# Moving a gate's sine and last multiplication into the even step of a pair of tiles

## Chip, cores and metric

One core of one Trainium2 chip runs the whole program. The metric is device time in microseconds (us) of one execution, as the median of several; lower is better. All data is float32.

## What is computed

The program is a cross attention between tokens and a small recurrent state, and behind it a two-layer network whose activation is h * cos(h). Cut to what matters:

```python
# x: (8, 8, 512, 64), state: (8, 8, 32, 64)
a  = softmax(scale * x @ state.T);  xread = a @ state
a2 = softmax(scale * state @ x.T);  sread = a2 @ x
y  = concat(xread, sread)                 # (8, 8, 544, 64)
y  = y.transpose(0, 2, 1, 3).reshape(4352, 512)
h  = y @ w_in                             # w_in: (512, 2048)
g  = h * cos(h)
out = g @ w_out                           # w_out: (2048, 512)
```

## The kernel before

**Tiles and steps.** The hidden layer is made in tiles of 128 hidden features by 512 tokens of one batch: 16 tiles `f` for each of the 8 batches `b`, and 16 smaller ones at the end for the state rows of all batches. One tile is one *step*; step 32 is tile 0 of batch 2. Steps 0 to 31 (batches 0 and 1) are ordered by a planner of their own. Everything from step 32 on is issued by the loop that starts at line 1676, which calls `later_pair` (line 1631) for each step, and it is this part that the change touches. Each engine works through its own queue strictly in the order in which the program issued the instructions; the order of the statements in `later_pair` therefore is the order of the work. A period is 32 steps (two batches), and its issue pattern repeats: 32 to 63, 64 to 95, 96 to 127.

**Hidden tiles in pairs, seven products.** Two neighbouring tiles (an even step and the odd one after it) form a pair and are made together by a Strassen-like scheme: seven products in place of eight, `seven_part` (line 531). A pair's seven products are issued as parts 0 to 3, two steps ahead of their use: at an even step TensorE (PE) does part 0 and part 1 of the *coming* pair, at the odd step part 2 and part 3. Behind part 0 ScalarE (ACT) makes two copies (lines 528, 529). VectorE (DVE) adds one sum after part 1 and one after part 2 (`seven_sum`, line 551; called the first and the second sum here). Part 2 can't start before the first sum is done, part 3 not before the second. There are two double banks of PSUM, so the coming pair is written where the pair before the current one was: its part 0 has to wait until that pair's last multiplication has read the bank.

**The gate.** h * cos(h) of a pair takes four instructions, each 128 x 1024: `gate` (ACT, line 564) rounds to an integer, `gate2` (DVE, line 567) subtracts, `gate3` (ACT, line 570) takes the sine, `gate4` (DVE, line 584) multiplies by h and writes to `g_all`. One buffer `q_all` carries all four, so the next pair's `gate` waits for this pair's `gate4`. Before the change `gate` and `gate2` stand in the even step, `gate3` and `gate4` in the odd one.

**The rest of a step.** Between the parts PE does one or two *stages* (`multiply`, line 772: eight matmul records for the output product, itself a seven-product scheme named p1 to p7 in stages 0 to 6), each followed by copies on ACT (lines 780, 781, 787) or sums on DVE (783, 789, 607). GpSimd (POOL) makes the sums of activations which these products read (`Product.sums`, `outer_sum`, line 715) and the sums of weight columns which part 0, 1 and 2 read (`sw_sums`, line 521). The *outer sums* that combine rows of activations are split between DVE and POOL; rows of the four blocks are numbered 0 to 3.

**Attention work between.** `plan(b)` puts the attention of the next batch and the *state products* (`products`, line 312, into the PSUM banks `at`, copied by ACT at line 462 to `sw_all`) into steps 0 to 15 of a batch: `go(0)` issues the PE part, `go(1)` and `go(2)` ACT copies, `go(3)` and `go(4)` DVE work, `go(5)` the exponentials. State products of a batch are made at its steps 0, 3, 8 and 12, `scores` (again into `at`) at step 4, `spread2` and `norm1` (DVE lines 373, 374, 332, 393) at step 8 and `halves` (DVE, line 507) at steps 12 and 13.

The names and lines that the change and the steps of the prediction touch: `later_pair` 1631 to 1673; `plan` 972 to 1015; the loop's outer sums 1699 and 1700; `gate` 564, `gate2` 567, `gate3` 570, `gate4` 584; `seven_copies` 528 and 529; `seven_sum` 551; `products_kept` 462.

Of the kernel before, what the change touches and what calls it, by code (L numbers as in the profile page):

```python
# [22 lines left out]
def kernel(  # L23
# [8 lines left out]
    nc = tc.nc  # L32
# [6 lines left out]
    NF = Dff // P  # L39
# [28 lines left out]
    QT, NQUAD = 4, 12  # L68
    g_all = consts.tile([P, (NQUAD + 1) * QT, S], F32)
    TEMPS = 4  # L70
    quads_free = [11]

    def quad(n):
        return g_all[:, QT * n:QT * n + QT]
# [392 lines left out]
    def part(b, name, *args):  # L467

        if b not in attn:
            attn[b] = Attention(b)  # L470
        getattr(attn[b], name)(*args)
        if (name, args) == ("reads", (1,)) and b + 1 < B:
            if b > 0:
                attn[b + 1] = Attention(b + 1)
                loads_due.extend(attn[b + 1].load_tokens())
            loads_due.extend(load_x(b + 1))
# [5 lines left out]
    def hidden(t):  # L482
        if t.paired:
            t.hp = h_pairs[t.at][:, t.f % 2, 0:t.n]
        else:
            t.hp = single_pool.tile([P, S], F32, name="h1")
        for i in range(t.kn):
            nc.tensor.matmul(out=t.hp, lhsT=t.lhs(i), rhs=t.rhs(i),  # L488
                             start=(i == 0), stop=(i == t.kn - 1))
# [8 lines left out]
    def seven(t):  # L498
        return t.pair is not None and t.b > 1
# [48 lines left out]
    def seven_sum(t, k):  # L548
        h1, h2 = [h_pairs[t.at][:, i] for i in range(2)]
        o = (h1, h2)[k][:, HI]  # L550
        nc.vector.tensor_tensor(o, h2[:, LO], sums_all[:, 0], op=ALU.add)  # L551
# [7 lines left out]
    def gate(t):  # L559
        t.q = q_all[:, t.f % 2, 0:t.n]  # L560
        if t.paired:
            t.hp = h_pairs[t.at][:, :, 0:t.n]
            t.q = q_all[:, :, 0:t.n]
        nc.scalar.activation(t.q.bitcast(I32), t.hp, func=ACTF.Copy, bias=0.25)  # L564

    def gate2(t):
        nc.vector.tensor_tensor(t.q, t.q.bitcast(I32), t.hp, op=ALU.subtract)  # L567

    def gate3(t):
        nc.scalar.activation(t.q, t.q, func=ACTF.Sin, bias=halfpi,  # L570
                             scale=-TWO_PI)

    def gate4(t):
        row = t.row
        if t.i // QT == len(quads_of[row]):
            quads_of[row].append(quads_free.pop(0))
        t.slot = QT * quads_of[row][t.i // QT] + t.i % QT
        t.g = g_all[:, t.slot, 0:t.n]
        g = t.g
        if t.paired:  # L580
            t.mate.slot = t.slot + 1
            t.mate.g = g_all[:, t.slot + 1, 0:t.n]
            g = g_all[:, t.slot:t.slot + 2, 0:t.n]
        nc.vector.tensor_tensor(g, t.hp, t.q, op=ALU.mult)  # L584
# [125 lines left out]
    def sub(engine, o, x1, x2):  # L710
        n = max(1, S // o.shape[2])
        if engine is nc.vector:
            n = o.shape[1]
        for i in range(0, o.shape[1], n):
            engine.tensor_tensor(o[:, i:i + n], x1[:, i:i + n], x2[:, i:i + n],  # L715
                                 op=ALU.subtract)
# [253 lines left out]
    warm(WARM, a0.xp[3])  # L970

    def plan(b):
        pe, x_act, y_act, x_dve, y_dve, z_act = [
            {s: [] for s in range(NF)} for _ in range(6)]

        def prod(s, b, nt, *bank):
            pe[s].append((b, "products", nt) + bank)
            x_act[s].append((b, "products_kept", nt) + bank)

        def pairs(s, b, name, kept, i):  # L980
            pe[s] += [(b, name, i), (b, name, i + 1)]
            x_act[s].append((b, kept, i))
            y_act[s].append((b, kept, i + 1))

        def early(b, s):
            for k in range(NK):
                to = (x_dve, y_dve)[k % 2]
                to[s[k // 2]].append((b, "tokens_turned", k))
            pe[s[2]].append((b, "scores"))
            x_dve[s[2]].append((b, "max1"))  # L990
            x_dve[s[3]].append((b, "spread1"))
            y_dve[s[3]].append((b, "shift"))
            y_dve[s[4] - 1].append((b, "max2"))
            z_act[s[4]].append((b, "exps"))
            y_dve[s[4]].append((b, "sums1"))
            x_dve[s[5]].append((b, "spread2"))
            y_dve[s[5]].append((b, "norm1"))

        def late(b, s):
            pairs(s[0], b, "turn", "turn_kept", 0)  # L1000
            pe[s[1]].append((b, "reads", 0))
            pe[s[2]].append((b, "reads", 1))
            x_dve[s[2]].append((b, "keep"))
            pe[s[3]].append((b, "keep2"))
            x_act[s[3]].append((b, "keep3"))

        if b:
            prod(0, b, 1)
            prod(3, b, 2)
            prod(8, b, 3)  # L1010
            if b + 1 < B:
                prod(12, b + 1, 0)
                early(b + 1, (1 + (b == 1), 2 + (b == 1), 4, 5, 7, 8, 9))
                late(b + 1, (9, 10, 11, 15))
        return pe, x_act, y_act, x_dve, y_dve, z_act


    all_tiles = list(tiles())
# [45 lines left out]
    def outer_sum(engine, n, o, x1, x2, half, i):  # L1064
        o, x1, x2 = [quad(quads_of[n, r][half])[:, 2 * i:2 * i + 2]
                     for r in (o, x1, x2)]
        sub(engine, o, x1, x2)
# [42 lines left out]
    def go(n):  # L1110
        for p in todo[n]:
            part(*p)
# [513 lines left out]
    def names_raw(i):  # L1626
        h = i % 2
        n = (2 * h, 2 * h + 1) if i < 4 else range(QT)
        return " ".join(f"Q{SLOTS[i]}_{k}" for k in n)

    def later_pair(step, t, ahead):
        coming = ahead[0] if ahead and ahead[0].paired else None
        seven_ = coming is not None and seven(coming)
        first = coming if even or coming is None else coming.mate
        if not t.paired:
            hidden(t)
        if even or not t.paired:
            gate(t)
        else:
            gate3(t.mate)  # L1640
            go(5)
        if seven_:
            seven_part(first, 0 if even else 2)
        elif coming is not None:
            hidden(coming)
        if even or not t.paired:
            gate2(t)
        if t.b == 1 and s in (13, 14):
            halves(2, s - 13)
        if seven_ and not even:  # L1650
            seven_sum(first, 1)
        if not t.paired:
            gate3(t)
        if not t.paired:
            gate4(t)
        elif not even:
            gate4(t.mate)
        if even:
            stages(step, 1)
        go(0)  # L1660
        if not even:
            stages(step, 1)
        if seven_:
            seven_part(first, 1 if even else 3)
            if even:
                seven_sum(first, 0)
        go(1)
        go(3)
        if t.pair is None and not even:
            state_sums(t.mate)  # L1670
            state_sums(t)
        go(2)
        go(4)

    first_pair()
    for step, t in enumerate(all_tiles[FIRST:], FIRST):
        s, even = step % NF, step % 2 == 0
        if s == 0 and t.b < B:
            steps = plan(t.b)
        todo = [p[s] if t.b < B else [] for p in steps]  # L1680
        while stores_due:
            stores_due.pop(0)()
        for u in all_tiles[step + 3:step + 4]:
            if seven(u) and u.f % 2 == 0:
                sw_sums(u)
        now[0] = step
        while totals_due and totals_due[0][0] <= step:
            totals_due.pop(0)[1]()
        if step == PERIOD:
            singles.__exit__(None, None, None)  # L1690
            pool2 = ctx.enter_context(tc.tile_pool(name="hps2", bufs=1,
                                                   space=PSUM))
            h_pairs[0] = pool2.tile([P, 2, S], F32, name="h2")
        later_pair(step, t, all_tiles[step + 2:step + 3])
        if later and later[0][0] <= step:
            later.pop(0)[1]()
        for what in weights_at[step]:
            what()
        for what in outer_at[step]:
            outer_sum(*what)  # L1700
        for pd, k in sums_at[step]:
            pd.sums(k)
        if t.b < B - 1 and t.b > 1 and s in (12, 13):
            halves(t.b + 1, s - 12)
        stages(step)
        load_now(H if step < NF else 4)
        if step == PERIOD * (B // 2) - 8:
            load_end_weights(2)
        if t.pair is None and t.n_th > 3 and len(quads_free) > 2:
            load_end_weights(1)  # L1710
# [36 lines left out]
```

## Time and profile before

| quantity | value |
|---|---|
| median of 3 runs | 740.53 us (739.6 to 740.9) |
| the profiled execution: its own time | 740.65 us |
| its span, first to last instruction | 738.9 us |
| PE matmul busy | 708.2 us, 96% |
| PE weight loads busy | 519.0 us, 70% |
| POOL busy | 542.5 us, 73% |
| DVE busy | 506.8 us, 69% |
| ACT busy | 347.3 us, 47% |
| mean granted TensorE clock | 0.993 |

The rows of the four gate instructions for pairs (48 each): line 564 ACT 1029 ns, line 567 DVE 1216 ns, line 570 ACT 1151 ns, line 584 DVE 1217 ns. A seven-product sum (line 551) is 430 ns, an outer sum on DVE (line 715, 128 x 1024) 1490 ns, a copy of a state product (line 462) 590 ns, a POOL sum of 128 x 512 1349 ns.

How to read it: the page gives busy time of each engine for the whole span, then in 40 slices, then a chain of work followed back from the end. The matmul records of PE overlap: a record of 256 columns lasts 381 ns on average, but eight of them follow each other in 1.73 us, so the distance from start to start is 0.22 us. A pause of less than about 0.2 us is thus not seen as idle time, and pauses have to be read from the start times in the timeline.

A step is found in the timeline by its `gate` (line 564, ACT, 128 x 1024), one for each even step: step 32 at 165.0 us, 36 at 185.1, 40 at 205.5, 42 at 214.8, 52 at 264.2, 60 at 302.1, 64 at 321.0, 72 at 363.2, 96 at 478.5, 116 at 579.3.

### The profile page before, as it was taken

How to read it: one execution, taken by the hardware profiler on the slowest of the kernel's cores; microseconds unless marked ns; L12 is line 12 of the kernel's file. 1: busy time of each engine (PE TensorE's matmuls, PEld its weight loads, DVE VectorE, ACT ScalarE, POOL GpSimd, SP SyncE). 2: the span in 40 equal slices, each digit the busy share in tenths (PEclk: the TensorE clock that was granted, in tenths of full speed). 3: DMA queues.
4: the chain of work that ended last, by engine and by line, in shares of the span. 5: the costliest groups of instructions: out<-in, count | busy, mean ns of one | idle time of the engine just before them, and what ended most of it. 6: DMA issues, size and time to landing. Idle time of an engine off the chain costs nothing.

```text
span 738.9 us, 10734 instructions
## 1 busy us (share of the span) xinstructions
PE 708.2 (96%) x3626; PEld 519.0 (70%) x3626; DVE 506.8 (69%) x703; ACT 347.3 (47%) x586; POOL 542.5 (73%) x524
## 2 busy tenths in 40 slices
PE   8898889999999999999999999999999999999997
PEld 3343343477778878777778788777688788888886
DVE  4989979957866668849756577768665467355550
ACT  5799675654463446343634464344634533211110
POOL 1557789375998997588998665879989665799600
PEclk9999999999999999999999999999999999999999
DMA  9966799536346964693238635762225466456662
GB/s 297 285 192 193 236 265 301 122 96 150 87 128 117 214 172 115 142 197 86 82 80 168 160 96 116 147 154 83 75 68 119 115 205 143 108 156 203 155 152 46
DMA packets 204021, 111.33 MB, mean 151 GB/s; under 512 B 149888, under 2 KB 166784, under 8 KB 203968
## 3 DMA queue, kind: packets, MB, share of 16 engines
q1 hardware_dynamic: 202880, 110.14, 57.4%
q8 instruction: 29, 0.48, 0.3%
q10 hardware_dynamic: 960, 0.39, 0.2%
q14 instruction: 24, 0.20, 0.1%
q0 software_dynamic: 128, 0.13, 0.1%
HBM read 87.03 MB, written 23.59 MB: 150 GB/s over the span
## 4 chain that ended last, share of the span: by engine, by line
PE 59%; POOL 21%; DVE 9%; issue 3%; DMA 3%; ACT 2%; SPq 1%; ACTq 0%; POOLq 0%; DVEq 0%
PE o L772 29%; POOL g_all L715 16%; PE h L543 13%; PE h L488 8%; POOL swS_all L521 3%; PE at L312 3%; PE at L877 2%; DMA held<-in_state_dram 2%; PE o L640 2%; POOL sw_all L521 2%; DVE g_all L715 1%; PE at L417 1%; DVE q_all L567 1%; DVE g_all L232 1%; DVE g_all L584 1%
## 5 line engine op out<-in xcount | busy, mean ns | idle before, releaser
L715 POOL TENSOR_TENSOR g_all<-g_all 128x512 f32<-128x512 f32 x252 | 332.5, 1349 | 61.8 <-DVE g_all L715 40.4
L772 PE MATMUL o<-g_all 128*128 128x256 f32 x1456 | 343.7, 381 | 2.4 <-POOL g_all L715 2.4
L772 PEld LDWEIGHTS o<-g_all 128*128 128x128 f32 x1456 | 273.7, 190 | 49.7 <-issue 5.7
L567 DVE TENSOR_TENSOR q_all<-q_all,h 128x1024 f32<-128x1024 int32 (+1 forms) x88 | 85.3, 971 | 40.7 <-ACT q_all L564 40.4
L564 ACT ACTIVATE q_all<-h 128x1024 int32<-128x1024 f32 (+1 forms) x88 | 73.1, 833 | 81.2 <-PE h L543 35.1
L584 DVE TENSOR_TENSOR g_all<-h,q_all 128x1024 f32<-128x1024 f32 (+1 forms) x88 | 85.7, 973 | 24.5 <-ACT q_all L570 23.6
L570 ACT ACTIVATE q_all<-q_all,halfpi 128x1024 f32<-128x1024 f32 (+1 forms) x88 | 84.2, 957 | 38.7 <-DVE q_all L567 38.5
L551 DVE TENSOR_TENSOR h<-h,sums_all 128x256 f32<-128x256 f32 x96 | 41.3, 430 | 77.5 <-PE h L543 60.2
L488 PE MATMUL h<-aT_all,sw_all 128*128 128x512 f32 x128 | 64.0, 628 | 13.0 <-DVE g_all L584 12.3
L543 PE MATMUL h<-aT_all,sw_all 128*128 128x256 f32 x192 | 59.6, 392 | 3.8 <-DVE g_all L584 3.4
L543 PE MATMUL h<-aS_all,swS_all 128*128 128x256 f32 x192 | 60.2, 395 | 2.6 <-ACT sums_all L529 1.8
L715 DVE TENSOR_TENSOR g_all<-g_all 128x1024 f32<-128x1024 f32 x42 | 62.0, 1490 | 0.1
L543 PE MATMUL h<-aS_all,sw_all 128*128 128x256 f32 x192 | 58.0, 384 | 0.1
L488 PEld LDWEIGHTS h<-aT_all,sw_all 128*128 128x128 f32 x128 | 23.2, 195 | 44.3 <-issue 21.5
L521 POOL TENSOR_TENSOR swS_all<-sw_all 128x128 f32<-128x128 f32 x48 | 22.5, 468 | 41.8 <-ACT sw_all L462 41.8
L543 PEld LDWEIGHTS h<-aS_all,swS_all 128*128 128x128 f32 x192 | 33.9, 189 | 27.0 <-issue 12.1
L780 ACT COPY o<-o 128x256 f32<-128x256 f32 x26 | 9.3, 357 | 85.1 <-PE o L772 85.1
L543 PEld LDWEIGHTS h<-aT_all,sw_all 128*128 128x128 f32 x192 | 34.5, 189 | 16.3 <-DVE g_all L584 12.2
L237 POOL TENSOR_TENSOR w_in<-w_in,aS_all 128x1024 int32<-128x1024 int32 (+1 forms) x10 | 22.3, 2241 | 29.9 <-DVE w_in L232 27.2
L787 ACT COPY o<-sums_all 128x256 f32<-128x256 f32 x26 | 9.8, 378 | 68.2 <-PE o L772 68.2
L543 PEld LDWEIGHTS h<-aS_all,sw_all 128*128 128x128 f32 x192 | 35.6, 190 | 8.2 <-DVE h L551 2.7
L607 DVE SCALAR_TENSOR_TENSOR held<-o,held 128x512 f32<-128x512 f32 x38 | 25.9, 681 | 13.7 <-PE o L772 13.1
(116 smaller groups left out, 931.6 us busy)
## 6 DMA issues: line engine op xcount, KB each, us to landing
g_all<-blocks_kept SPq DMA_DIRECT2D x206, 256.0 KB, 2.8
blocks_kept<-g_all SPq DMA_DIRECT2D x48, 256.0 KB, 3.9
g_all<-in_moe_w_out_dram SPq DMA_DIRECT2D x8, 1024.0 KB, 5.7
out_dram<-ot SPq DMA_DIRECT2D x128, 64.0 KB, 2.0
g_all<-in_moe_w_in_dram SPq DMA_DIRECT2D x6, 1024.0 KB, 7.1
x_b<-in_x_dram SPq DMA_DIRECT2D x24, 256.0 KB, 4.7
xT<-in_x_dram SPq DMA_DIRECT2D x80, 64.0 KB, 2.8
x_b<-in_x_dram SPq DMA_DIRECT2D x16, 128.0 KB, 4.3
```

Of the source, the lines that this page charges most:

```text
L237: nc.gpsimd.tensor_tensor(bits, bits, e, op=ALU.add)
L488: nc.tensor.matmul(out=t.hp, lhsT=t.lhs(i), rhs=t.rhs(i), start=(i == 0), stop=(i == t.kn - 1))
L521: nc.gpsimd.tensor_tensor(o, x1, x2, op=op)
L543: nc.tensor.matmul(out=out_, lhsT=w, rhs=r, start=start, stop=True, skip_group_check=True)
L551: nc.vector.tensor_tensor(o, h2[:, LO], sums_all[:, 0], op=ALU.add)
L564: nc.scalar.activation(t.q.bitcast(I32), t.hp, func=ACTF.Copy, bias=0.25)
L567: nc.vector.tensor_tensor(t.q, t.q.bitcast(I32), t.hp, op=ALU.subtract)
L570: nc.scalar.activation(t.q, t.q, func=ACTF.Sin, bias=halfpi, scale=-TWO_PI)
L584: nc.vector.tensor_tensor(g, t.hp, t.q, op=ALU.mult)
L607: nc.vector.scalar_tensor_tensor(out=out.t[:, ch], in0=bank, scalar=TWO_PI, in1=b.t[:, ch], op0=ALU.mult, op1=ALU.add)
L715: engine.tensor_tensor(o[:, i:i + n], x1[:, i:i + n], x2[:, i:i + n], op=ALU.subtract)
L772: nc.tensor.matmul(out=o, lhsT=ring[(self.first + k) % NB][:, i], rhs=g[:, i], start=(start and i == 0), stop=(i == QT - 1), skip_group_ch ...
```

## The change

The sine and last multiplication of a pair move from the odd step into the even one, behind part 1 and the first sum of the coming pair, provided that the coming pair is one of the seven-product kind and that a buffer for the result is at hand (`fits`). They do not move at steps 32, 40, 48 and 52, nor for the last pair before the state tiles (126) and in the state tiles. Where they move, DVE's outer sums that read row 3 are put off from the even step to the odd one, behind the second sum (in every period one such sum of step 2 and one of step 4 of the period). ACT's copies of state products made at an odd step (tile 3 of each batch) move to the next step, behind that step's `gate` and seven-product copies.

In the emitted program PE, POOL and the DMA queues keep their order; only DVE and ACT are reordered. The number of instructions is the same, activation table loads included. Since `gate4` takes its buffer one step earlier, some buffers of `g_all` are handed out in another order.

```diff
@@ plan
         def prod(s, b, nt, *bank):
             pe[s].append((b, "products", nt) + bank)
-            x_act[s].append((b, "products_kept", nt) + bank)
+            (w_act[s + 1] if s % 2 else x_act[s]).append(
+                (b, "products_kept", nt) + bank)
@@ later_pair
+        early = t.paired and seven_
         if even or not t.paired:
             gate(t)
         else:
-            gate3(t.mate)
+            if not t.mate.gated:
+                gate3(t.mate)
             go(5)
         if seven_:
             seven_part(first, 0 if even else 2)
...
         if even or not t.paired:
             gate2(t)
+        go(6)
...
         elif not even:
-            gate4(t.mate)
+            if not t.mate.gated:
+                gate4(t.mate)
+            while sums_late:
+                outer_sum(*sums_late.pop(0))
         if even:
             stages(step, 1)
         go(0)
...
             seven_part(first, 1 if even else 3)
             if even:
                 seven_sum(first, 0)
+        fits = t.pair is not None and (t.i % QT > 0 or len(quads_free) > 1)
+        t.gated = even and early and fits
+        if t.gated:
+            gate3(t)
+            gate4(t)
         go(1)
         go(3)
@@ the loop over steps
         for what in outer_at[step]:
-            outer_sum(*what)
+            if t.gated and what[0] is nc.vector and 3 in what[2:5]:
+                sums_late.append(what)
+            else:
+                outer_sum(*what)
```

More of the change, by code (lines that the diff above doesn't have):

```diff
@@ L972, in plan @@
     def plan(b):
-        pe, x_act, y_act, x_dve, y_dve, z_act = [
-            {s: [] for s in range(NF)} for _ in range(6)]
+        pe, x_act, y_act, x_dve, y_dve, z_act, w_act = [
+            {s: [] for s in range(NF)} for _ in range(7)]
         def prod(s, b, nt, *bank):
             pe[s].append((b, "products", nt) + bank)
-            x_act[s].append((b, "products_kept", nt) + bank)
+            (w_act[s + 1] if s % 2 else x_act[s]).append(
+                (b, "products_kept", nt) + bank)
         def pairs(s, b, name, kept, i):
@@ L1014, in plan @@
                 late(b + 1, (9, 10, 11, 15))
-        return pe, x_act, y_act, x_dve, y_dve, z_act
+        return pe, x_act, y_act, x_dve, y_dve, z_act, w_act
     all_tiles = list(tiles())
@@ L1629, in names_raw @@
         return " ".join(f"Q{SLOTS[i]}_{k}" for k in n)
+    sums_late = []
     def later_pair(step, t, ahead):
```

## The prediction, made before the changed kernel ran

> **What bounds the kernel now.** I read the slices first (PE at nine tenths from step 32 on), then the waits, then the chain of waits between 173 and 218 us, then the timeline of four places. PE is full by the page, but its records overlap, so I took start-to-start distances above 0.22 us as pauses. PE starts of part 0 that come late behind `gate4` (line 584) are the pauses the change aims at:
>
> ```profile
> PE h L543 <- DVE g_all L584: 3.4, 8, 0.4
> PEld h L543 <- DVE g_all L584: 12.2, 24, 0.8
> ACT q_all L564 <- DVE g_all L584: 28.2, 9, 5.2
> ```
>
> The columns are total us, times, longest. The second row, weight loads, counts overlapped time as well, so I don't add it. From the timeline, part 0 is late by 0.18, 0.28, 0.59, 0.09, 0.59, 0.10 and 0.59 us in the first period (steps 34, 36, 38, 40, 42, 54, 62), by 0.19, 0.27, 0.59, 0.59, 0.59 in the second (66, 68, 70, 74, 94), by 0.19, 0.28, 0.59, 0.59 in the third: 6.3 us in all, 0.8% of the span. That is the most this change can remove by its main idea, and about 0.1 us more for each, which the trace shows PE to lose on restarting after a pause.
>
> Most of these lie in steps 34 to 42 of a period, where POOL and DVE are full as well. The chain there:
>
> ```profile
> 176.75 6.87 POOL g_all L715 x4
> ...
> 204.46 10.83 POOL g_all L715 x8
> 215.29 0.42 POOL swS_all L521
> 215.71 0.04 issue
> 215.75 0.70 PE h L543 x2
> ```
>
> POOL works from 176.75 to 215.71 without a pause and PE then waits for its weight sums: in the first period POOL sets when step 42 goes on, whatever DVE does. POOL's start at 176.75 waits for DVE's first outer sum of step 33.
>
> At the end of a period, steps 60 to 62, the bound is DVE alone (its rows of the timeline):
>
> ```profile
> 304.45 1.22 DVE L567 TENSOR_TENSOR q_all<-q_all,h 128x1024 f32<-128x1024 int32 x1
> ...
> 307.14 1.22 DVE L715 TENSOR_TENSOR g_all<-g_all 128x1024 f32<-128x1024 f32 x1
> 308.27 0.42 DVE L507 TENSOR_TENSOR aS_all<-aT_all 128x256 f32<-128x256 f32 x1
> 308.73 1.37 DVE L507 TENSOR_TENSOR aS_all<-aT_all,aS_all 128x256 f32<-128x256 f32 x1
> 310.02 0.68 DVE L607 SCALAR_TENSOR_TENSOR held<-o,held 128x512 f32<-128x512 f32 x1
> 310.62 0.42 DVE L551 TENSOR_TENSOR h<-h,sums_all 128x256 f32<-128x256 f32 x1
> 310.96 1.21 DVE L584 TENSOR_TENSOR g_all<-h,q_all 128x1024 f32<-128x1024 f32 x1
> ```
>
> DVE is full; part 3 (PE 311.10) waits for the second sum (310.62 to 311.04), then part 0 of step 62 (PE 312.22) for `gate4`. And step 52, where the scores (line 312) need the banks that the moved copies (line 462) empty:
>
> ```profile
> 263.27 1.07 ACT L462 COPY sw_all<-at 128x512 f32<-128x512 f32 x2
> ...
> 264.21 1.06 ACT L564 ACTIVATE q_all<-h 128x1024 int32<-128x1024 f32 x1
> 265.13 0.41 ACT L528 COPY h<-h 128x256 f32<-128x256 f32 x1
> ...
> 265.57 0.37 ACT L529 COPY sums_all<-h 128x256 f32<-128x256 f32 x1
> ...
> 265.64 1.09 PE L312 MATMUL at<-xT,st_all 64*32 64x512 f32 x16
> ```
>
> **What the Trainium skill says.** "SBUF — State Buffer", section Who interferes with whom: a DVE instruction with two SBUF inputs contends with a GpSimd one that reads SBUF, and one blocks fully. The trace agrees: POOL's 128x512 sums take 1.27 us alone and 2.19 to 2.26 beside a DVE outer sum or `norm1`. The number of such meetings does not change, so I price this at nothing, with 1 us either way in the range. "ScalarE: Activation LUTs", What ACT_TABLE_LOAD costs: about 1283 ns; the trace has 1.28 us. No load is added, but those at steps 56, 72, 88, 104 now stand in front of a sine that DVE needs a step earlier (taken at its 1.28 us). "Perfetto Trace Analysis", Identifying the Most-Contended Engine: matmul busy share is a poor measure; hence the start distances.
>
> **The change part by part.** I walk the queues with the trace's durations: in a full DVE queue one instruction costs about 1.13 us for a gate part, 0.33 for a seven-product sum, 0.6 for 128x512, 1.1 to 1.4 for an outer sum.
>
> *First period, steps 34 to 42.* POOL's start hangs on step 33, whose pair isn't moved, and its run is full: 0. (If DVE got later than POOL, a loss of up to 0.5.)
>
> *Second and third period, steps 64 to 74* (times of the second). `gate4` of step 64 moves to step 64, so the token transposes of step 65 follow its second sum at 330.3 in place of 332.0, and the outer sum that starts POOL comes 1.6 us earlier, at 331.5. POOL is then ready 1.6 us earlier at step 74. Pauses at 66, 68, 70 go. New ones: scores of step 68 wait for the moved copies (0.2), and the second sum of step 71 stands behind sine-bound `gate4` and the two maxima of step 70: it ends at 359.7 while part 3 could start at 359.0 (0.8 late); stage p6 2 waits 0.3 for a copy behind the sine. Part 0 of step 72 comes at 360.3 (now 360.7). ACT reaches the exponentials at 357.4 (now 359.4), so `gate` of step 72 starts at 361.2 (now 363.2), and the pause before part 1 (0.56) goes. But then `gate4` waits for copy, table load and sine (365.85), and only behind it come `spread2` and `norm1`, 3.94 us as in 366.62 to 370.55, then a 0.33 us sum: second sum 371.3 to 371.7 (now 370.9 to 371.3), part 3 at 371.8 in place of 370.05. Part 0 follows at once, the next stage at 373.2, now 373.99. Gain 0.8 us, in each of the two periods (third: 0.8). Bounds: 1.6 gained (POOL's limit) to 1.2 lost (if `gate` of step 72 comes no earlier than now).
>
> *Copies moved, steps 52 and 84.* `gate` starts at 263.27, the copies behind lines 528 and 529 then end about 266.0; scores, ready at 265.65, lose 0.35 each: +0.7. In step 52 `gate4` isn't moved, so step 54's sine and `gate4`, in front of two maxima, push the second sum of 55 to 281.2 against a part 3 due at 280.85: +0.45 with the restart. Steps 57 and 89 have `gate4` in front of `norm1` as well: +0.2 each, +0.4. At step 116 no scores follow, and the pause before part 1 (581.16, line 529 late behind the copies) goes: -0.64.
>
> *Steps 60 and 92.* `gate4` goes in front of outer sum, halves and line 607: 1.13 us more in front of the second sum, which ends at 312.2. Part 3 starts at 312.25 in place of 311.10, then part 0 at once, the next stage at 313.65 in place of 313.19: the wait of 0.69 us (0.59 and the restart) is gone, but a serial part 3 comes in: +0.46 each, +0.9. What hides here is nothing: DVE is full from 304.45 on.
>
> *Steps 46, 78, 110.* `gate4` before a transpose and line 607 puts the second sum to 243.75, part 3 due at 243.57; the 0.12 pause before part 2 goes: +0.1 each, +0.3. *Other steps* (42, 44, 50, 58, 80): DVE waits for PE there (idle 0.3 to 2.5 us in front of line 551), which hides the moved instruction; without that cover each would cost 1.1. Step 42 of the first period: its `gate4` comes from step 40, not moved: 0.
>
> *What moves along.* PE, POOL and the DMA queues keep their order, and no DMA is issued elsewhere. `gate4` takes its buffer a step earlier, but only where a second one is free, so it doesn't get the one freed last: 0. POOL's column sums behind the copies that now follow a sine (line 462, 1.15 us later at 44, 56, 80) keep about a step until part 0 needs them: 0, and 0.5 each if that cover is gone.
>
> Sum: -1.6 + 0.7 + 0.45 + 0.4 - 0.64 + 0.9 + 0.3 = +0.5 us. On the profiled execution's own 740.65 us (1.75 more than its span) that is 741.15; the median of the runs is 0.1 below that execution, so 741.0.
>
> **The rivals.** *DVE's order costs more than it frees* (slower): one mechanism, a full DVE queue with `gate4` in front of the second sum, at step 72 and 104 above all. If `gate` of step 72 starts at 362.0 rather than 361.2, the 0.8 us is gone; if it starts as now, each period loses 1.2: 741.0 + 1.6 = 742.6 to 741.0 + 4.0 = 745.0; I take 743.5. For it: DVE idles about 1 us before each `gate4` that waits for its sine in a full stretch. Against: ACT is 47% busy and comes earlier by the walk. *The waits go and nothing comes in their place* (faster): periods two and three gain POOL's 1.6 each, steps 62 and 94 0.7 each, step 116 0.64: -5.2, with the scores' +0.7 -4.5, so 740.5 - 4.5 = 736.0; half of it 738.3; I take 737.4. For it: DVE 69% busy, and most gates have slack. Against: DVE is full exactly where the waits are. *Nothing reaches PE in the full stretch* (POOL's run ends as before in every period): then the two periods lose their 0.8, 742.6, slower by little; the outer sum of step 65 being 1.6 us earlier speaks against it.
>
> **How the numbers follow.** What a measurement of this kernel can tell from no change is about 0.2%, 1.5 us. The balance of the walk is the likeliest, 0.42, its own range 738.5 to 743.3 by the bounds of step 72 and the 1 us for POOL's meetings; the full-DVE rival has 0.26, POOL's 0.08, the free waits 0.24. The range reaches into the others on both sides: 737.6 to 744.2. Slower by over 1.5 us (above 742.0) are nearly all of the full-DVE rival, half of POOL's and a sixth of the balance: 0.36; faster (below 739.0) most of the free waits and a little of the balance: 0.24; the rest, 0.40, within.
>
> **What would show it.** Right: no part 0 late behind line 584 at steps 36, 38, 62, 68, 70; part 3 late behind line 551 at steps 61, 73, 93, 105; scores late behind line 462 at 52 and 84; POOL's run after step 65 starting 1.6 us earlier relative to part 2 of that step. Wrong: part 3 on time at step 61 or 73 (the fast rival), or `gate` of step 72 no earlier against part 0 than now (the slow one).

## The result, and the profile after

Below, *before* and *after* are the two kernels. The kernel after is slower: 747.13 us median of 7 runs (745.1 to 751.9) against 739.79 us, a ratio of 1.0109 with a 95% interval of 1.0089 to 1.0129. The prediction was 741.0 us with a range of 737.6 to 744.2. The profiled execution took 745.3 us, span 743.5.

The waits at which the change aimed are all but gone from the profile after (total us, times, longest), and others stand in their place:

```profile
PEld h L543 <- DVE h L551: 13.8, 15, 2.2
PE h L543 <- DVE h L551: 10.3, 16, 1.8
...
ACT q_all L564 <- DVE g_all L584: 2.4, 2, 1.7
...
PEld h L543 <- DVE g_all L584: 1.6, 3, 0.8
...
PE h L543 <- DVE g_all L584: 0.4, 1, 0.4
```

The rows with L584 answer to 3.4, 12.2 and 28.2 us before. But parts 2 and 3, which read what a seven-product sum (L551) writes, now stand still for 10.3 us (before, PE has no such row), and the longest of those pauses is 1.8 us.

**Where the time goes.** Both traces hold the same 3626 matmul records in the same order, so each can be compared with its counterpart. I call the start of a record after the change less its start before the *lag*. It is -1.27 us at step 32 (steps 0 to 31 were not touched; that is how two executions differ) and 4.66 at the end, so steps 32 to 127 cost 5.9 us. Its growth, stretch by stretch (numbers without a word are steps), beside the terms of the prediction's sum:

| stretch | predicted, us | lag grows by, us |
|---|---|---|
| steps 32 to 44 | 0 | +0.66 |
| 46, 78, 110 | +0.1 each | +0.53, +0.54, +0.53 |
| scores of 52 and 84 | +0.35 each | +0.64, +0.54 |
| part 3 of 55; of 87 | +0.45; 0 | +0.54; +0.56 |
| 57, 89 | +0.2 each | +0.17, +0.17 |
| 60 to 64, 92 to 96 | +0.46 each | +0.46, +0.46 |
| 64 to 76, 96 to 108 | -0.8 each | +0.50, +0.49 |
| 116 to 119 | -0.64 | -0.75 |
| elsewhere | 0 | -0.1 |
| sum | +0.5 | +5.9 |

The largest miss is 64 to 76. VectorE's rows of the timeline after, steps 69 to 71, and last ScalarE's `gate` of step 72 (start, duration, instruction; in brackets idle time before it and its releaser):

```profile
352.00 0.42 DVE L551 TENSOR_TENSOR h<-h,sums_all 128x256 f32<-128x256 f32 x1
352.33 1.95 DVE L715 TENSOR_TENSOR g_all<-g_all 128x1024 f32<-128x1024 f32 x1
354.21 0.68 DVE L607 SCALAR_TENSOR_TENSOR held<-o,held 128x512 f32<-128x512 f32 x1
...
357.27 1.21 DVE L567 TENSOR_TENSOR q_all<-q_all,h 128x1024 f32<-128x1024 int32 x1
358.40 0.43 DVE L551 TENSOR_TENSOR h<-h,sums_all 128x256 f32<-128x256 f32 x1
359.70 1.23 DVE L584 TENSOR_TENSOR g_all<-h,q_all 128x1024 f32<-128x1024 f32 x1 [0.87 <-ACT q_all L570]
...
364.07 1.02 ACT L564 ACTIVATE q_all<-h 128x1024 int32<-128x1024 f32 x1
```

The outer sum that was put off takes 1.95 us beside a POOL sum (the other five of steps 65 to 68 take 1.18 to 1.47), so `gate2` (357.27), the first sum of step 70 (358.40) and the sine behind `gate2` come late. Then DVE, full until then, stands idle for 0.87 us because `gate4` waits for that sine, and everything behind waits with it. At step 72 and 73 the same again, DVE and PE rows:

```profile
367.99 0.43 DVE L551 TENSOR_TENSOR h<-h,sums_all 128x256 f32<-128x256 f32 x1 [1.64 <-PE h L543]
368.78 1.22 DVE L584 TENSOR_TENSOR g_all<-h,q_all 128x1024 f32<-128x1024 f32 x1 [0.36 <-ACT q_all L570]
369.93 0.97 DVE L373 TENSOR_SCALAR i_all<-i_all 128x34 f32<-128x34 f32 x1
...
372.61 1.50 DVE L393 TENSOR_TENSOR aT_all<-aT_all,xT 128x1024 f32<-128x1024 f32 x1
374.03 0.42 DVE L789 TENSOR_TENSOR o<-o,sums_all 128x256 f32<-128x256 f32 x1
374.37 0.42 DVE L551 TENSOR_TENSOR h<-h,sums_all 128x256 f32<-128x256 f32 x1
...
374.84 0.70 PE L543 MATMUL h<-aS_all,sw_all 128*128 128x256 f32 x2 [1.76 <-DVE h L551]
```

`gate4` stands in front of `spread2`, `norm1` and the second sum. The chain of 4 us behind it can't start before 369.93, and part 3 starts at 374.84 with PE idle for 1.76 us. Before the change the chain began straight behind the first sum (366.62).

### The profile page after: what moved, and what is told of

Same layout as the page of the kernel before. It is cut to its first block, busy times and chain, and to the rows that moved or that the text cites. A ratio compares the mean times of both kernels' runs of the same rounds, so it can differ in the third digit from the quotient of the medians.

```text
span 743.5 us, 10708 instructions
## 1 busy us (share of the span) xinstructions
PE 709.7 (95%) x3626; PEld 522.2 (70%) x3626; DVE 507.2 (68%) x703; ACT 346.7 (47%) x586; POOL 543.0 (73%) x524
## 5 line engine op out<-in xcount | busy, mean ns | idle before, releaser
L584 DVE TENSOR_TENSOR g_all<-h,q_all 128x1024 f32<-128x1024 f32 (+1 forms) x88 | 85.7, 974 | 27.6 <-ACT q_all L570 27.4
L551 DVE TENSOR_TENSOR h<-h,sums_all 128x256 f32<-128x256 f32 x96 | 41.1, 428 | 69.3 <-PE h L543 59.2
L488 PE MATMUL h<-aT_all,sw_all 128*128 128x512 f32 x128 | 65.5, 640 | 11.3 <-DVE g_all L584 10.6
L543 PE MATMUL h<-aS_all,sw_all 128*128 128x256 f32 x192 | 59.1, 390 | 10.3 <-DVE h L551 10.3
L543 PE MATMUL h<-aT_all,sw_all 128*128 128x256 f32 x192 | 57.4, 381 | 0.4 <-DVE g_all L584 0.4
L488 PEld LDWEIGHTS h<-aT_all,sw_all 128*128 128x128 f32 x128 | 23.4, 196 | 42.3 <-issue 22.0
L543 PEld LDWEIGHTS h<-aT_all,sw_all 128*128 128x128 f32 x192 | 36.3, 190 | 6.8 <-DVE g_all L584 1.6
```

Of the source, the lines that this page charges most:

```text
L488: nc.tensor.matmul(out=t.hp, lhsT=t.lhs(i), rhs=t.rhs(i), start=(i == 0), stop=(i == t.kn - 1))
L543: nc.tensor.matmul(out=out_, lhsT=w, rhs=r, start=start, stop=True, skip_group_check=True)
```

## The theories and the experiments

Theory 1: the loss is the order on VectorE, the early `gate4` in front of a seven-product sum where the queue is full. Theory 2: it is the moved copies of state products and ScalarE's order. Theory 3: the outer sums put off collide with POOL. Theory 4: longer pauses of PE set off half-clock stretches, which would also explain times up to 751.9. Each kernel was timed in five rounds beside the kernel before; a ratio is to those runs, with its 95% interval. "From step 32" is the growth of the lag in the one profile of each. What they gave:

| run | median, us | before, us | ratio | from step 32, us |
|---|---|---|---|---|
| a_again | 746.95 | 739.77 | 1.0093 (1.0076 to 1.0111) | +6.9 |
| sine_only | 739.44 | 739.77 | 0.9992 (0.9981 to 1.0003) | 0.0 |
| no_copies | 747.33 | 739.77 | 1.0101 (1.0083 to 1.0118) | +6.1 |
| no_defer | 746.89 | 739.77 | 1.0096 (1.0079 to 1.0113) | +7.3 |
| copies_only | 740.70 | 740.51 | 1.0002 (0.9991 to 1.0013) | +0.9 |
| skip_full | 738.81 | 740.51 | 0.9974 (0.9963 to 0.9984) | -1.8 |
| only_full | 743.55 | 739.65 | 1.0054 (1.0037 to 1.0071) | +4.4 |
| full_and_4 | 749.23 | 739.46 | 1.0123 (1.0106 to 1.0140) | +9.4 |
| late_mul | 742.23 | 739.65 | 1.0029 (1.0020 to 1.0037) | +2.0 |
| v1a | 735.07 | 740.51 | 0.9929 (0.9912 to 0.9946) | -5.1 |
| v1b | 738.51 | 740.51 | 0.9978 (0.9968 to 0.9988) | -1.6 |
| v1f | 733.89 | 739.65 | 0.9912 (0.9898 to 0.9926) | -5.3 |
| v1g | 733.02 | 739.46 | 0.9910 (0.9896 to 0.9925) | -6.3 |

### The change again, and each part alone

**a_again**: the kernel after with a blank line more (its line numbers are higher by one).

> The kernel after, once more, with its profile. All theories: about 747 us (745 to 752). Theory 1 (VectorE's full queue: the last multiplication waits for its sine in front of the two seven-product sums) expects the same pauses of TensorE behind the line of seven_sum (L551, 9 to 11 us in all) in the profile. Theory 4 (the spread above 745 comes from TensorE's clock: half-clock windows of 3.4 us set off by the longer pauses) expects more such windows in a profile of a longer execution, one for each 1.7 us lost, and in the pair steps; if there are three of them as before and all in the first 100 us, theory 4 falls.

The same time, and nearly the same pauses behind the sums (8.9 us, a little less than the 9 to 11 expected). Its lag grows by 1.0 us more than in the first profile. The stretch 32 to 44 costs 0.23 here in place of 0.66: at step 42 PE waits 1.67 us for POOL, and the pauses behind DVE at 39 and 41 are mostly gone, so this term depends on the execution. One place that no theory named, just before step 52, has 1.2 us more. Its waits between 253 and 257 us:

```profile
PEld o L773 <- DMA g_all<-blocks_kept: 1.4, 1, 1.4
PE o L773 <- DMA g_all<-blocks_kept: 1.0, 1, 1.0
```

A block of weights lands late. The early `gate4` of step 46 pushes the transpose L615 from 240.68 (before) to 241.81 us (profile after), the store of that result starts on the queue of SP, the engine that issues the transfers, at 242.54 in place of 241.59, and the fetches of blocks stand behind it. That is not all of it: the run sine_only, where this `gate4` is not early, has 1.0 us there too, and the first profile of the kernel after has none. The fetches take 3.3 to 4.1 us to landing before, 3.6 to 4.8 here, 3.5 to 6.0 in sine_only. There is no stretch at half the TensorE clock behind step 32 in this profile.

**sine_only**

```diff
         if t.gated:
             gate3(t)
-            gate4(t)
...
-            if not t.mate.gated:
-                gate4(t.mate)
+            gate4(t.mate)
```

> After, but the last multiplication of the gate stays in the odd step, where it was; the sine stays early, the outer sums put off and the copies late. Theory 1 (the last multiplication in front of the sums is what costs): L551 pauses fall back to near 0, the part-0 waits behind L584 come back in full (about 7 us of them), time 739 to 742 us. Theory 2 (the moved copies of state products and the order of ScalarE cost): still at least 3 us above before, 744 or more. Theory 3 (the outer sums put off collide with GpSimd's sums): 743 or more, since they are still put off.

With the early multiplication alone taken back, the loss is gone, although sine, copies and outer sums stay moved. Theories 2 and 3 as the main cause fall here. Its waits:

```profile
PE h L543 <- DVE g_all L584: 2.3, 5, 0.5
PE h L543 <- DVE h L551: 1.4, 3, 0.7
```

The L551 pauses are down from 10.3 to 1.4 us. I had expected the part-0 waits back in full; they are not (2.3, before 3.4), since the outer sum no longer stands in front of `gate4` in the odd step. That hint led to the kernels v1a and v1g.

**no_copies** (copies of state products left where they were) and **no_defer** (outer sums left in the even step):

```diff
-            (w_act[s + 1] if s % 2 else x_act[s]).append(
-                (b, "products_kept", nt) + bank)
+            x_act[s].append((b, "products_kept", nt) + bank)
```
```diff
-            if t.gated and what[0] is nc.vector and 3 in what[2:5]:
+            if False:
```

> After, with the copies of state products left in the odd step where they were. Theory 1: within 1.5 us of after, 745 to 749 us; the scores' waits behind L462 at the steps 52 and 84 (0.35 us each) go. Theory 2: back to before, 739 to 742 us. Theory 3: as after.

> After, with VectorE's outer sums left in the even step, so behind the early last multiplication and in front of the odd step's seven-product sum. Theory 1: slower than after by 1 to 3 us (748 to 752), since 1.5 us more stands in front of the second sums in the full steps. Theory 3: faster than after by at least 2 us (743 or less), since the collisions with GpSimd's sums (1.95 us for one outer sum where 1.5 is its time alone) go. Theory 2: as after.

Neither changes the time by more than its interval. In no_defer the lag grows by +0.66, +0.50 and +0.50 in the three stretches 32 to 44, 64 to 76, 96 to 108, the same as after: an outer sum behind the second sum of step 69 holds up the first sum of step 70, and left in step 68 it holds up the second sum of 69 by as much. The 1 to 3 us that theory 1 expected for it were wrong: putting off is worth nothing either way. In no_copies the scores' waits of 52 and 84 are gone and the lag falls by 0.46 in 96 to 108, but PE's pauses at part 3 of 73 and 105 get longer (2.20 us from start to start beyond the usual 0.22, after 1.92), one is followed by a half-clock stretch (1.6 to 1.7 us, below), and blocks of weights land late before 52 and 84 (1.0 and 0.5). So the time stays.

**copies_only**: before, with that one edit of the copies.

> Before, with only the copies of state products moved into the even step after them. Theory 1 (VectorE's full queue): within 1 us of before, 739 to 740.5; a wait of 0.35 us of the scores behind L462 at the steps 52 and 84, part of which the block's own inner pause of 0.4 us absorbs. Theory 2 (the copies): 743 or more, already unlikely after the run without them.

No difference in time. The trace shows the price of the copies cleanly: +0.65 at step 52, +0.54 at 84, -0.62 at 116.

### Which places, and idle time or the multiplication itself

**skip_full** and **only_full** divide the early pairs: positions 6, 8, 12, 14 of each batch, which I took for the places where DVE is fullest, and the others. Both leave the copies where they were before the change.

```diff
-        t.gated = even and early and fits
+        t.gated = even and early and fits and s not in (6, 8, 12, 14)
```
```diff
-        t.gated = even and early and fits
+        t.gated = even and early and fits and s in (6, 8, 12, 14)
```

> After, but the pairs at the positions 6, 8, 12 and 14 of each batch (steps 38, 40, 44, 46, 54, 56, 60, 62 and so on) keep sine and last multiplication in the odd step, and the copies stay where they were. Theory 1, in its narrow form (only where VectorE's queue is full does the early last multiplication hold up a sum): the L551 pauses of 1 to 2 us at part 3 of the steps 41, 61, 73, 93 and 105 go, the part-0 waits behind L584 at 36, 68, 70, 100 and 102 stay gone, 738 to 740 us. Wide form (every early last multiplication costs by the other moves it makes): 742 or more.

> The complement of the run skip_full: sine and last multiplication early only at the positions 6, 8, 12 and 14 of each batch, copies where they were. Theory 1 (narrow): all of the loss and more, 746 to 749 us, since skip_full alone gains 1 to 2 us and the two should add up to after's 747; the pauses behind L551 as in after, the part-0 waits behind L584 at 36, 68 and 70 back. If the two don't add up within 2 us, the places act on one another.

skip_full is 0.26% faster than before: the early gate is right where DVE has slack. The lag falls by 1.67 in 64 to 76 and by 0.96 in 96 to 108. only_full is slower, but by 4 us and not by the 6 to 9 expected: the halves add up to about 2 us, after costs 7. The lag of only_full grows by 0.01 in each of 64 to 76 and 96 to 108, so the early pairs at 70 and 72 cost nothing there by themselves, only together with the earlier ones.

**full_and_4**: only_full with position 4 as well (`s in (4, 6, 8, 12, 14)`).

> As the kernel of the run only_full, with position 4 of each batch (steps 36, 52, 68, 84 and so on) early as well. It tells why the halves don't add up: only_full costs 4 us and skip_full gains 1.9, together 2.1, but after costs 7. If the rest comes from step 68 being early (its outer sum is put off past the second sum of step 69 and then stands, at 1.95 us where it collides with GpSimd, ahead of step 70's first sum): 1.4 us more in each of two or three periods, less 0.3 for the wait at 68, so 745.5 to 747.5 us, with part 2 of step 71 late behind L551 again. If it comes from step 66 or from the other early positions: as only_full, 743 to 744 us.

749.23 us, at least as slow as after and above the 745.5 to 747.5 expected. So two early pairs in a row, 68 and 70, act on one another, as the text above expected; in the profile the half clock below and a block of weights that lands 0.6 us late before step 52 come on top. VectorE's timeline at step 69 shows how, and then PE's at step 73:

```profile
353.19 0.42 DVE L551 TENSOR_TENSOR h<-h,sums_all 128x256 f32<-128x256 f32 x1
353.52 2.29 DVE L715 TENSOR_TENSOR g_all<-g_all 128x1024 f32<-128x1024 f32 x1
...
359.94 0.43 DVE L551 TENSOR_TENSOR h<-h,sums_all 128x256 f32<-128x256 f32 x1
```
```profile
376.66 0.70 PE L543 MATMUL h<-aS_all,sw_all 128*128 128x256 f32 x2 [2.04 <-DVE h L551]
377.19 0.91 PE L543 MATMUL h<-aT_all,sw_all 128*128 128x256 f32 x2
377.90 1.06 PE L543 MATMUL h<-aS_all,swS_all 128*128 128x256 f32 x2
378.75 2.88 PE L772 MATMUL o<-g_all 128*128 128x256 f32 x8
```

The outer sum put off past the second sum takes 2.29 us beside POOL, and the first sum of step 70 is late. In 96 to 108 the lag grows by 1.24 where only_full has 0.01, close to the 1.4 expected; in 64 to 76 by 2.92, because there PE, idle for 2.04 us, goes on at half clock. PEclk, the granted clock, in the answer by windows (us, busy time and records of PE, PEld, DVE, ACT, POOL, then the clock):

```profile
376.00:377.50 1.50, 0.84 (x4) 0.71 (x5) 1.19 (x3) 1.12 (x3) 1.34 (x4) 0.94 0.36 135
377.50:379.80 2.30, 2.30 (x7) 1.85 (x6) 1.22 (x1) 1.74 (x4) 2.30 (x3) 0.50 0.00 0
379.80:382.00 2.20, 2.20 (x15) 1.64 (x15) 0.33 (x1) 1.11 (x1) 2.20 (x3) 0.78 0.00 0
```

**late_mul**: after, with the early `gate4` moved to the end of the even step, where its sine has long been done.

```diff
         if t.gated:
             gate3(t)
-            gate4(t)
...
         go(4)
+        if t.gated:
+            gate4(t)
```

> After, but the early last multiplication comes at the very end of the even step on VectorE, so its sine has long been there; it still stands in front of the odd step's second sum. This splits theory 1 in two. 1a (VectorE stands idle for the sine, 0.87 us at step 70 and like it elsewhere, and that idle time is the loss): L551 pauses shrink by about 0.9 us at each of the places of 1 to 2 us, time 741 to 743 us. 1b (the 1.21 us of the multiplication itself in front of the second sum is the loss, whatever it waits for): L551 pauses within 0.3 us of those of after, time 745 to 748 us.

742.23 us: 1a, idle time in front of the sine-bound `gate4`, is right for about two thirds of the loss. Same rows as above, steps 72 and 73:

```profile
367.25 0.43 DVE L551 TENSOR_TENSOR h<-h,sums_all 128x256 f32<-128x256 f32 x1 [1.16 <-PE h L543]
367.59 0.58 DVE L373 TENSOR_SCALAR i_all<-i_all 128x34 f32<-128x34 f32 x1
...
371.61 1.21 DVE L584 TENSOR_TENSOR g_all<-h,q_all 128x1024 f32<-128x1024 f32 x1
372.74 0.42 DVE L789 TENSOR_TENSOR o<-o,sums_all 128x256 f32<-128x256 f32 x1
373.07 0.42 DVE L551 TENSOR_TENSOR h<-h,sums_all 128x256 f32<-128x256 f32 x1
```

`spread2` fills the time in which DVE stood idle for the sine. The stretches fall to -0.09, -0.42 and -0.60 and part 3 of 55 and 87 costs nothing: together 3.9 us less than after (0.75 + 0.92 + 1.09 + 1.10). What stays unchanged, 46, 78, 110 (+0.53 each) and 60, 92 (+0.46 each), is the multiplication itself in front of a sum.

### Versions that beat both

**v1a** leaves the gates as before and moves only what stood in front of `gate4`: VectorE's outer sums of the even step go behind it in the odd step, and one goes a step earlier (first changed line).

```diff
-                ((27, 28), dve, 0, 2, 0, 1),
+                ((27, 27), dve, 0, 2, 0, 1),
...
-                ((34, 34 + (not end)), dve, 0, 3, 0, 1),
-                ((35, 36), dve, 2, 3, 2, 1),
+                ((34 + (not end),) * 2, dve, 0, 3, 0, 1),
+                ((35, 36 + (not end)), dve, 2, 3, 2, 1),
...
             gate4(t.mate)
+            for what in outer_at[step]:
+                if what[0] is nc.vector:
+                    outer_sum(*what)
+            outer_at[step] = [x_ for x_ in outer_at[step]
+                              if x_[0] is not nc.vector]
```

> Before with its gates untouched; VectorE's outer sums of the even steps go into the odd step behind the last multiplication (so behind the second sum and the gate), and the one that stood ahead of the token transposes one step earlier. Theory 1 says that what made the last multiplication late in before was the outer sum (1.49 us) ahead of it on VectorE, so the part-0 waits behind L584 of 0.6 us each at 38, 68, 70, 100 and 102 go and no L551 wait comes: 737 to 739 us. Theory 3 (outer sums that are put off collide with GpSimd's) expects 740.5 or more.

735.07 us, better than expected. VectorE at step 37 in the timeline before, then in that of v1a:

```profile
190.95 1.45 DVE L715 TENSOR_TENSOR g_all<-g_all 128x1024 f32<-128x1024 f32 x1
...
192.93 0.42 DVE L551 TENSOR_TENSOR h<-h,sums_all 128x256 f32<-128x256 f32 x1
193.26 1.21 DVE L584 TENSOR_TENSOR g_all<-h,q_all 128x1024 f32<-128x1024 f32 x1
```
```profile
191.89 0.43 DVE L551 TENSOR_TENSOR h<-h,sums_all 128x256 f32<-128x256 f32 x1 [0.17 <-PE h L543]
192.23 1.21 DVE L584 TENSOR_TENSOR g_all<-h,q_all 128x1024 f32<-128x1024 f32 x1
193.36 1.22 DVE L715 TENSOR_TENSOR g_all<-g_all 128x1024 f32<-128x1024 f32 x1
```

The sum and `gate4` come first, the outer sum, for which nothing waits so soon, after them. The lag falls by 1.0 in each of the three full stretches and at 60 and 92, and the L551 waits that come up are 0.25 us each.

**v1b** sends `spread2` and `norm1` behind `gate4` too; **v1f** does so for the even batches' pair at position 8 alone and moves the turn and both reads a step later; **v1g** is v1f with both reads in one step. The turn is a transpose of the attention weights, the reads are the products with them. From v1g's edit:

```diff
+            if b % 2 == 1:
+                w_dve[s[5] + 1].append((b, "spread2"))
+                w_dve[s[5] + 1].append((b, "norm1"))
+                return
             x_dve[s[5]].append((b, "spread2"))
             y_dve[s[5]].append((b, "norm1"))
...
-                late(b + 1, (9, 10, 11, 15))
+                late(b + 1, (9, 10, 11, 15) if b % 2 else (10, 11, 11, 15))
```

> As the kernel of the run v1a, and spread2 and norm1 (L373, L393) also go from the even step of a pair to the odd step behind the last multiplication. Theory 1: the part-0 waits at 42, 74 and 106 go as well, 736 to 738.5 us; if the normalised tokens come too late for their consumer, a wait behind L393 takes their place and the time is that of v1a or more.

> As the kernel of the run v1a; in addition spread2 and norm1 (L373, L393) go behind the last multiplication in the pairs at position 8 of the even batches alone (steps 40, 72, 104), and the turn of the attention weights (L400, L405) and the reads after it move one step later there, so that ScalarE's copy L405 no longer stands waiting in front of L529. Theory 1: the waits at 42, 74 and 106 (0.24 + 0.59 us each) go and nothing comes in their place, 2.5 us below v1a: 732 to 733.5 us. If a later consumer (reads, L417) waits instead: 735 or more.

> As the kernel of the run v1f, except that both reads (L417) of the even batches' attention come in the odd step 43 (75, 107), before the next products take their bank, so that the numbers are those of the reference. Theory 1: the L551 and L584 waits at 42, 74 and 106 stay gone; the wait for GpSimd's sum swS_all (L521) of 1.4 us that v1f showed in their place at 211.9 stays as well, so 0.3 to 0.6 us a period below v1a: 733.5 to 735 us. A wait behind the copies of the turned weights (L405), now directly ahead of both reads, would make it 735 or more.

v1b gives back most of v1a's gain: ScalarE's copy L405 waits for `norm1` in front of the copy L529, and L529 makes PE late by 1.1 us at 42, 58, 74, 90 and 106. The text had named a wait behind `norm1`, and the time as v1a's or more if it came. In v1f the second reads share a bank with the next state products, so part of the attention is computed from other numbers; its time only bounds the next one. v1g has neither fault: 733.02 us, 0.90% below before (0.75 to 1.04) and just below the 733.5 to 735 expected (v1f, at 733.89, came just above its 732 to 733.5). Its pauses at step 42 are now POOL's, in its timeline:

```profile
201.73 9.89 POOL L715 TENSOR_TENSOR g_all<-g_all 128x512 f32<-128x512 f32 x8
211.56 0.47 POOL L521 TENSOR_TENSOR swS_all<-sw_all 128x128 f32<-128x128 f32 x1
```
```profile
212.09 0.70 PE L543 MATMUL h<-aS_all,swS_all 128*128 128x256 f32 x2 [1.21 <-POOL swS_all L521]
```

The eight sums take 9.89 us (10.87 in the timeline before, where `norm1` runs beside them), and PE waits for the weight sums behind them.

## Why the prediction was wrong

- *Second and third period, steps 64 to 74, gain 0.8 us each*: the step that failed. Measured +0.50 and +0.49, 1.3 us off in each. POOL's run after step 65 did start 1.6 us earlier, as walked (334.54, less the lag of 1.75 at step 64, against 334.45), but DVE did not keep up. Less that lag, the second sum of step 71 ended at 360.7 (walked 359.7), `gate` of step 72 started at 362.3 (361.2), its `gate4` at 367.0 (365.85) and part 3 of step 73 at 373.1 (371.8). The term at fault is the one put at nothing because the number of meetings with POOL does not change: one outer sum of DVE started while a POOL sum was running and took 1.95 where the walk had 1.1 to 1.4, ahead of `gate2` and the first sum of step 70, so the sine came late. The lateness costs time because `gate4` waits for its sine (0.87 us idle at step 70, 0.36 at step 72) in front of the sums that PE needs; the walk had these waits, but with an earlier sine. late_mul shows this second half: there `gate` of step 72 is as late (363.82, less a lag of 1.37, is 362.4) and the outer sum takes 2.14, yet the two stretches gain 0.42 and 0.60, so without the wait for the sine 0.9 and 1.1 of the 1.3 us come back. That the outer sum is what made DVE late is read from the timeline and was not tried alone.
- The slower rival had this mechanism, a full DVE queue with `gate4` in front of a sum, and the idle microsecond as its argument, with 362.0 as the point from which `gate` of step 72 decides; the runs decide for it. At 742.6 to 745.0 it too was priced too low, since it left the other terms as they were. Its sign, `gate` of step 72 no earlier against part 0 than now, did not show: `gate` comes 1.0 us behind part 0 (2.5 before), because part 0 is late as well.
- *Steps 60 and 92 +0.46, step 116 -0.64, steps 57 and 89 +0.2, step 55 +0.45*: right, measured +0.46, -0.75 (of it -0.62 at 116 itself), +0.17, +0.54. The place and the kind of the new waits (part 3 late behind L551 at 61, 73, 93, 105; scores late behind L462) were all as written.
- *First period 0, POOL's run is full*: +0.66 in the first profile. POOL's run ends as before (213.99, less the lag of -1.27, against 215.29), but DVE got later than POOL at steps 39 and 41, the case put in brackets at 0.5. In a_again the stretch costs 0.23.
- *Steps 46, 78, 110, +0.1 each*: +0.53 each, a term that was mis-sized. The pause before part 2 was to go; it grew by 0.36 us, and part 3, behind a `gate4` that waits 0.28 us for its sine, is late by 0.17.
- *Scores lose 0.35 each*: 0.64 and 0.54; 0.35 was the wait of the first record alone. *Step 87*, for which the walk had nothing: +0.56, as at step 55.
- *No DMA is issued elsewhere*, so 0: SP's order is the same, but a store waits for a DVE transpose behind the moved `gate4`, and fetches wait behind the store. The block before step 52 costs 0 to 1.3 us, by execution; I had not priced it. In the profiles it is late by at most 0.2 us where the gates are as before (before, copies_only and the four v1 kernels) and by 0 to 1.3 in the nine others, but sine_only has no early `gate4` there; how much of it is the change's is open.
- *6.3 us of waits that can go* was right as a size. skip_full keeps only some of it (-1.8); v1a takes 5.1 with no gate moved.

The first profile is of an execution of 745.3 us, and its 5.9 us explain most of the 7.3 between the medians; a_again's 6.9 stand against 7.2. That the times of the first comparison reach 751.9 is not settled. Half-clock stretches are a candidate: the mean granted clock was 0.988 and 0.990 in the two longest executions (751.9 and 750.0) and 0.991 to 0.993 in the other five. But 0.004 of the clock is, by my estimate, 6 us at half clock and 3 us lost, of the 6.6 between 745.3 and 751.9, and neither of the two profiles of this kernel has such a stretch behind step 32.

## What to carry to other kernels

When an instruction on a full in-order queue is late, first move what stands in front of it and has time (here outer sums, worth 5 us), before moving the instruction itself earlier: an early instruction that must wait for its input stops the queue, and the one behind it may be what the bound engine needs. Put a waiting instruction where its input is already there, and let other work fill the time (late_mul got back 3.9 of 5.9 us by that). When a queue is re-ordered, follow each result to the stores and fetches behind it, even where the DMA order is unchanged.

## What the hardware showed

- A VectorE outer sum of 128 x 1024 took 1.18 to 2.30 us in the profiles before and after. The Trainium skill, "SBUF — State Buffer", section Who interferes with whom, says which pair of instructions does this; the sizes are from these traces. What counts is which of the two started first: the sum at 352.33 (after) started 0.87 us before the end of a POOL sum and took 1.95, the POOL sum took its usual 1.28. The sum at 334.4 started first and took 1.22, and the POOL sum beside it 2.19.
- PE fell to half clock behind a pause of 2.04 us, for 3.4 us, a loss of 1.6 to 1.7 us (seven records of 0.43 us in place of 0.22 us, and part of an eighth). The Trainium skill, "TensorE: Matmul & The Clock Gate", Part 1: The HAM clock gate, has the clock go cold after an idle window of about 3.4 us; here less was enough. In all the profiles the clock changes only at multiples of 3.41 us from its first change, and what these traces show fits a rule on such stretches. Of four pauses of that length in no_copies and full_and_4, two lie whole inside one stretch (373.92 to 377.33 in full_and_4, 371.94 to 375.36 in no_copies; 2.04 us idle in each) and were followed by half clock. The two that a boundary cuts, with 1.80 and 1.23 us idle in the fuller stretch, were not. Between 165 and 625 us no other stretch of any profile had more than 1.7 us idle, and none was followed by half clock. These are few cases, and no run was made to try it.
- The landing of one 256 KB block of weights before step 52 decided over 0 to 1.3 us from one execution to the next.
